# A gated scan and two MLPs on one core: the order of the SBUF tiles, and with it the offset at which each one begins

## The chip, the cores and the metric

The kernel runs on one core of a Trainium2 chip. The metric is the time of one execution on the device in microseconds (us), the median of repeated runs. SBUF, the memory that the engines read from and write to, has 128 partitions; a tile has the same address in each of them, and an address here is a number of bytes from the beginning of a partition.

## The reference

`x` and `f_logit` are `[2, 6080, 256]`; taken as rows there are 12160 tokens of 256 numbers. The weights are `[256, 2048]` and `[2048, 256]` for each of two MLPs, all in float32.

```python
def reference(x, f_logit, lower_bound, w_in1, w_out1, w_in2, w_out2):
    f = lower_bound + (1 - lower_bound) * sigmoid(f_logit)
    for t in range(S):                       # a scan along the 6080 tokens
        h = f[:, t] * h + (1 - f[:, t]) * x[:, t]
        y[:, t] = h
    x = y.reshape(12160, 256)
    x = square(relu(x @ w_in1)) @ w_out1     # first MLP
    return elu(x @ w_in2) @ w_out2           # second MLP
```

## The kernel before

**Precision.** Each float32 operand of a product is split into a high part and a low part, and a product is made of three matmuls: high weights with high data, high weights with low data, low weights with high data. Each of these is one load of 128x128 weights (the stationary operand, a run of 128 float32, 512 bytes, in each partition) and one matmul that streams 512 columns of data past them (the moving operand, 2048 bytes in each partition; 384 or 448 columns at some places near the beginning). The program has 8688 such pairs.

**Units and runs.** The tokens are cut into units, the first two smaller than the rest, which have 1024 tokens in two halves of 512. A run is one MLP on one unit; the first MLP of a unit goes two units ahead of the second. A run has eight slots, one for each eighth of the hidden dimension. From the third unit on, a slot has seven products for two halves of tokens and two halves of the hidden slice, with sums and differences of data and weights in place of the eighth product:

- `add_first`: three products, 9 matmuls, with weights from a tile `ws` and data from a tile `xa`;
- `add_later`: four products, 12 matmuls, with weights from `ws` and data from a tile `xb`;
- `add_out`, twice: 12 matmuls each (line 855), with weights from `wo0` or `wo1` (the output weights of the two MLPs, which stay in SBUF from the beginning) and data from a tile `g`.

The matmuls of `add_first` and `add_later` have one line in the profile, 633. The first two units of the first MLP are "plain": four products of 3 matmuls each for a half, with weights that lie alternately in a `ws` tile and in an `s` tile (`plain_weights`, line 321).

**Other engines.** Between the matmuls, ScalarE (ACT) and VectorE (DVE) copy products out of PSUM, add them, apply the activation and split the result into the parts in `g` (lines 652 to 678, 756 to 807). DVE also does the scan (line 602) and what leads to it (lines 575 to 589). The weights are split once, in the first quarter of a millisecond, and are kept in DRAM (`wd`); `ws` is reloaded from there for each slot (line 472). All DMAs but the very first go through the queue of SyncE.

**Order.** The class `Order` is a planner: it simulates the steps with fixed costs and writes them out, engine by engine. It knows nothing of addresses.

**Addresses.** Pools get their space in the order in which they are opened (lines 178 to 194), from low addresses to high. At the bottom lie 1024 bytes of scratch and four constants, a 32-byte place for each, up to byte 1152. Then come the two buffers of `ws` (7168 bytes each), then the pool `const` with five small tiles (`lb`, `ga`, `gb`, `carry`, `warm`, one 32-byte place each) and with `wo0` and `wo1` (32768 bytes each), then all the others. The sizes of all large tiles are multiples of 512 bytes. So all of them behind the small ones have the same remainder when their address is divided by 512, and so have all the slices of weights and of data that matmuls read, since these begin at multiples of 512 bytes in their tiles.

Of the kernel before, what the change touches and what calls it, by code (L numbers as in the profile page):

```python
# [7 lines left out]
F32 = mybir.dt.float32  # L8
F32R = mybir.dt.float32r
# [6 lines left out]
P = 128  # L16
HN = 512
CN = 256
SIZES = ((512, 384), (512, 512))
LEAD = 2  # L20
BEHIND = 2
AGE = 8.0
ROW = 1 / 2240
# [3 lines left out]
BUFS = {  # L27
# [3 lines left out]
}  # L31
# [119 lines left out]
def kernel(  # L151
# [12 lines left out]
    B, S, D = x.shape  # L164
# [3 lines left out]
    KF = DFF // P  # L168
# [6 lines left out]
    PLAIN = len(SIZES)  # L175
    starts = [sum(map(sum, units[:u])) for u in range(NU)]

    pools = {"ws": ctx.enter_context(tc.tile_pool(name="ws_pool", bufs=BUFS["ws"]))}
    const = ctx.enter_context(tc.tile_pool(name="const", bufs=1))
    lb = const.tile([P, KD], F32, name="lb")  # L180
    ga = const.tile([P, KD], F32, name="ga")
    gb = const.tile([P, KD], F32, name="gb")
    carry = const.tile([P, KD], F32, name="carry")
    warm = const.tile([P, 1], F32, name="warm")
    wo = [const.tile([P, KF, 2, D], F32R, name=f"wo{m}") for m in range(2)]
    pools |= {
        tag: ctx.enter_context(tc.tile_pool(name=f"{tag}_pool", bufs=n))
        for tag, n in BUFS.items()
# [27 lines left out]
    def slots_of(m, u):  # L216

        if not plain(m, u):
            return [(m, u, None, g) for g in range(KG)]
        a, b = ([(m, u, h, g) for g in range(KG)] for h in range(2))  # L220
        got = a[:LEAD]
        for i in range(LEAD, KG + LEAD):
            got += a[i : i + 1] + b[i - LEAD : i - LEAD + 1]
        return got

    runs = [(0, u) for u in range(BEHIND)]
    for u in range(BEHIND, NU):
        runs += [(1, u - BEHIND), (0, u)]
    runs += [(1, u) for u in range(NU - BEHIND, NU)]
    slots = [s for r in runs for s in slots_of(*r)]  # L230
# [25 lines left out]
    for s in slots:  # L256
        m, u, h, g = s
# [702 lines left out]
    for kind, s in pe_order:  # L960
# [3 lines left out]
        m, u, h, g = s  # L964
        if kind != "later" and s == first_of[m, u]:
            if m == 0:
                keys = {}
                before = slots_of(0, u - 1)
                for hh in range(2):
                    due = in_due[(m, u, hh, 0) if plain(m, u) else s]  # L970
                    for q in range(2):
                        k = before[SCANS[2 * hh + q] * len(before) // KG] if u >= BEHIND else None
                        keys[hh, q] = add_scan(n_scan, u, hh, q, due - 6.0 + 2.0 * (q - 1), n_first[k] if k else None)
# [43 lines left out]
```

## Time and profile before

| | us |
|---|---|
| median of 3 runs | 2049.47 (2049.08 to 2049.62) |
| profiled execution, its own time | 2049.94 |
| its span, first to last instruction | 2048.2 |
| TensorE (PE) busy | 1995.6 |
| weight loads (PEld) busy | 1633.5 |
| VectorE (DVE) busy | 1676.1 |
| ScalarE (ACT) busy | 1638.2 |

The busy time of PE is the time in which at least one matmul is under way; consecutive matmuls overlap, so it doesn't say how fast they follow one another. That is read from a timeline: from the start of a block of matmuls to the start of the next block, divided by the number of matmuls in it. In the timeline used below, the second column of a row (the block's length) runs to the end of its last matmul and overlaps with the next block; the first column is the one to subtract.

### The profile page before, as it was taken

How to read it: one execution, taken by the hardware profiler on the slowest of the kernel's cores; microseconds unless marked ns; L12 is line 12 of the kernel's file. 1: busy time of each engine (PE TensorE's matmuls, PEld its weight loads, DVE VectorE, ACT ScalarE, POOL GpSimd, SP SyncE). 2: the span in 40 equal slices, each digit the busy share in tenths (PEclk: the TensorE clock that was granted, in tenths of full speed). 3: DMA queues.
4: the chain of work that ended last, by engine and by line, in shares of the span. 5: the costliest groups of instructions: out<-in, count | busy, mean ns of one | idle time of the engine just before them, and what ended most of it. 6: DMA issues, size and time to landing. Idle time of an engine off the chain costs nothing.

```text
span 2048.2 us, 24509 instructions
## 1 busy us (share of the span) xinstructions
PE 1995.6 (97%) x8688; PEld 1633.5 (80%) x8688; DVE 1676.1 (82%) x2285; ACT 1638.2 (80%) x2170; POOL 0.2 (0%) x4
## 2 busy tenths in 40 slices
PE   5999969999999999999999999999999999999998
PEld 4887958888888888888888888888888888888886
DVE  6878997788889779879878888977987987857886
ACT  6988967887888788888788788878888878878885
POOL 0000000000000000000000000000000000000000
PEclk9999989999999999999999999999999999999999
DMA  7877744324324334333432432433433333233231
GB/s 191 240 245 241 230 129 128 131 91 142 125 94 137 99 132 131 111 131 114 128 131 90 143 125 93 137 99 131 132 110 132 114 108 131 91 111 118 94 105 54
DMA packets 235138, 267.30 MB, mean 131 GB/s; under 512 B 160008, under 2 KB 160776, under 8 KB 235016
## 3 DMA queue, kind: packets, MB, share of 16 engines
q1 hardware_dynamic: 234432, 265.21, 41.3%
q8 instruction: 68, 1.11, 0.2%
q10 hardware_dynamic: 584, 0.53, 0.1%
q14 instruction: 54, 0.44, 0.1%
HBM read 221.91 MB, written 43.78 MB: 130 GB/s over the span
## 4 chain that ended last, share of the span: by engine, by line
PE 90%; DVE 4%; ACT 2%; DMA 2%; issue 1%; SPq 1%; DVEq 0%; ACTq 0%
PE a L855 47%; PE c L633 43%; DVE g L678 1%; DMA a<-rd 1%; DMA fs<-in_f_logit_dram 1%; ACT g L673 1%; SPq L566 0%; ACT r L658 0%; ACT a L369 0%; DMA st<-in_moe_w_in_dram 0%; ACT r L725 0%; DVE a L375 0%; DVE a L378 0%; DVE F L602 0%; DVE a L339 0%
## 5 line engine op out<-in xcount | busy, mean ns | idle before, releaser
L855 PE MATMUL a<-g,wo 128*128 128x512 f32 (+1 forms) x4608 | 1107.1, 389 | 0.9 <-DVE g L678 0.9
L855 PEld LDWEIGHTS a<-g,wo 128*128 128x128 f32 x4608 | 865.2, 188 | 184.5 <-DVE g L678 1.3
L678 DVE TENSOR_TENSOR g<-r,g 128x1024 fp32r<-128x1024 f32 (+2 forms) x384 | 463.2, 1206 | 169.4 <-ACT g L673 168.4
L633 PE MATMUL c<-xb,ws 128*128 128x512 f32 (+2 forms) x2208 | 540.4, 393 | 0.0
L673 ACT ACTIVATE g<-r 128x1024 fp32r<-128x1024 f32 (+2 forms) x384 | 403.4, 1050 | 134.7 <-PE a L855 121.8
L633 PEld LDWEIGHTS c<-xb,ws 128*128 128x128 f32 x2208 | 414.7, 188 | 94.2
L633 PE MATMUL c<-xa,ws 128*128 128x512 f32 (+1 forms) x1680 | 427.6, 398 | 44.2 <-ACT xa L482 35.7
L633 PEld LDWEIGHTS c<-xa,ws 128*128 128x128 f32 x1680 | 318.1, 190 | 122.1 <-ACT xa L482 36.1
L756 ACT ACTIVATE s<-c 128x512 f32<-128x512 f32 (+1 forms) x528 | 307.3, 588 | 7.3 <-PE c L633 7.3
L668 DVE SCALAR_TENSOR_TENSOR r<-e,r 128x1024 f32<-128x1024 f32 (+1 forms) x192 | 232.1, 1209 | 34.3 <-ACT e L665 34.3
L662 ACT ACTIVATE e<-r 128x1024 f32<-128x1024 f32 (+1 forms) x192 | 201.5, 1049 | 39.8 <-DVE r L800 37.0
L658 ACT ACTIVATE r<-r 128x1024 f32<-128x1024 f32 x192 | 201.7, 1051 | 2.3
L665 ACT ACTIVATE e<-e 128x1024 f32<-128x1024 f32 (+1 forms) x192 | 201.4, 1049 | 1.5
L796 ACT ACTIVATE r<-c 128x512 f32<-128x512 f32 (+1 forms) x176 | 104.0, 591 | 106.1 <-PE c L633 106.0
L760 DVE TENSOR_TENSOR s<-s 128x512 f32<-128x512 f32 (+1 forms) x176 | 119.9, 681 | 74.2 <-ACT s L756 74.0
L793 DVE TENSOR_TENSOR s<-c,s 128x512 f32<-128x512 f32 (+1 forms) x176 | 120.6, 685 | 39.9 <-PE c L633 38.9
L804 DVE TENSOR_TENSOR r<-c,s 128x512 f32<-128x512 f32 (+1 forms) x176 | 119.5, 679 | 4.4
L800 DVE TENSOR_TENSOR r<-c,s 128x512 f32<-128x512 f32 (+1 forms) x176 | 119.8, 680 | 2.2
L807 DVE TENSOR_TENSOR r<-s 128x512 f32<-128x512 f32 (+1 forms) x176 | 119.1, 677 | 0.0
L652 ACT ACTIVATE r<-r 128x1024 f32<-128x1024 f32 x80 | 84.4, 1055 | 3.5 <-DVE r L807 3.5
L655 ACT ACTIVATE r<-r 128x512 f32<-128x512 f32 x80 | 50.4, 630 | 30.7 <-DVE r L800 30.7
L602 DVE TENSOR_TENSOR_SCAN F<-fT,carry,xT 128x256 f32<-128x256 f32 (+2 forms) x94 | 65.3, 723 | 1.2
(47 smaller groups left out, 759.0 us busy)
## 6 DMA issues: line engine op xcount, KB each, us to landing
ws<-wd SPq DMA_DIRECT2D x176, 896.0 KB, 4.9
fs<-in_f_logit_dram SPq DMA_DIRECT2D x184, 64.0 KB, 2.4
xs<-in_x_dram SPq DMA_DIRECT2D x184, 64.0 KB, 2.5
xd<-o SPq DMA_DIRECT2D x46, 256.0 KB, 4.3
F<-xd SPq DMA_DIRECT2D x22, 512.0 KB, 5.0
out_dram<-o SPq DMA_DIRECT2D x88, 128.0 KB, 2.8
st<-in_moe_w_out_dram SPq DMA_DIRECT2D x16, 512.0 KB, 5.5
wd<-wp SPq DMA_DIRECT2D x24, 256.0 KB, 3.6
```

Of the source, the lines that this page charges most:

```text
L633: nc.tensor.matmul(out, lhsT=ws[:, p, w], rhs=xs[:, r, v], start=start and q == 0, stop=stop and q == 2, skip_group_check=check,)
L658: nc.scalar.activation(r_t[0], r_t[0], AF.Square)
L662: nc.scalar.activation(t["e"], r_t[0], AF.Relu, scale=-1.0)
L665: nc.scalar.activation(t["e"], t["e"], AF.Exp, scale=-1.0)
L668: nc.vector.scalar_tensor_tensor(r_t[0], t["e"], 1.0, r_t[0], op0=ALU.subtract, op1=ALU.max)
L673: nc.scalar.activation(g_t[s, which][:, 0], r_t[0], AF.Copy)
L678: nc.vector.tensor_tensor(g_t[s, which][:, 1], r_t[0], g_t[s, which][:, 0].bitcast(F32), op=ALU.subtract)
L756: nc.scalar.activation(t["s"][:, c - 1], t[c], AF.Copy)
L760: nc.vector.tensor_tensor(t["s"][:, 1], t["s"][:, 1], t["s"][:, 2], op=ALU.add)
L793: nc.vector.tensor_tensor(t["s"][:, 0], t[0], t["s"][:, 0], op=ALU.add)
L800: nc.vector.tensor_tensor(odd[0][:, 1], t[2], t["s"][:, 0], op=ALU.add)
L855: nc.tensor.matmul(a, lhsT=y, rhs=v, start=begin and jj == 0 and p == 0, stop=end and jj == len(mine) - 1 and p == 2, skip_group_check=True,)
```

## The change

The order in which the pools are opened is changed, and a tile of 56 float32 (224 bytes) that nobody uses is added behind the small constants. `wo0` and `wo1` get a pool of their own.

```diff
+GAP = 56
...
-    pools = {"ws": ctx.enter_context(tc.tile_pool(name="ws_pool", bufs=BUFS["ws"]))}
     const = ctx.enter_context(tc.tile_pool(name="const", bufs=1))
     lb = const.tile([P, KD], F32, name="lb")
     ga = const.tile([P, KD], F32, name="ga")
     gb = const.tile([P, KD], F32, name="gb")
     carry = const.tile([P, KD], F32, name="carry")
     warm = const.tile([P, 1], F32, name="warm")
-    wo = [const.tile([P, KF, 2, D], F32R, name=f"wo{m}") for m in range(2)]
+    const.tile([P, GAP], F32, name="gap")
+    pools = {"ws": ctx.enter_context(tc.tile_pool(name="ws_pool", bufs=BUFS["ws"]))}
+    outer = ctx.enter_context(tc.tile_pool(name="outer", bufs=1))
+    wo = [outer.tile([P, KF, 2, D], F32R, name=f"wo{m}") for m in range(2)]
```

The addresses in the two built programs, with the remainder by 512 in brackets:

| tile | before | after |
|---|---|---|
| small tiles | 15488 to 15616 | 1152 to 1280 |
| `ws`, two buffers | 1152 (128), 8320 (128) | 1536 (0), 8704 (0) |
| `wo0`, `wo1` | 15648 (288), 48416 (288) | 15872 (0), 48640 (0) |
| `xa`, `xb` (data of line 633) | 113952 (288), 126240 (288) | 114176 (0), 126464 (0) |
| `g`, two buffers (data of line 855) | 167200 (288), 175392 (288) | 167424 (0), 175616 (0) |
| `s`, two buffers | 183584 (288), 189728 (288) | 183808 (0), 189952 (0) |
| all other large tiles | (288) | (0) |

Apart from addresses the two programs are the same: the same instructions stand in the same order on every engine and every queue.

## Rows read from the trace of the kernel before

**Rows 1.** The page: busy time by engine; granted clock; the chain's shares by engine.
```profile
PE 1995.6 (97%) x8688; PEld 1633.5 (80%) x8688; DVE 1676.1 (82%) x2285; ACT 1638.2 (80%) x2170; POOL 0.2 (0%) x4
...
PEclk9999989999999999999999999999999999999999
...
PE 90%; DVE 4%; ACT 2%; DMA 2%; issue 1%; SPq 1%; DVEq 0%; ACTq 0%
```

**Rows 2.** Busy time by stretch: length, engines, then clock, DMA share, GB/s.
```profile
core 0: us, PE busy (x) PEld busy (x) DVE busy (x) ACT busy (x) POOL busy (x), PEclk, DMA share, GB/s
...
37.50:262.00 224.50, 221.54 (x1045) 192.90 (x1044) 189.58 (x319) 197.13 (x311) 0.00 (x0) 1.00 0.77 233
262.00:287.00 25.00, 8.02 (x21) 5.79 (x21) 24.88 (x44) 12.71 (x18) 0.00 (x0) 0.59 0.40 102
287.00:2033.50 1746.50, 1746.50 (x7565) 1420.65 (x7564) 1429.15 (x1866) 1408.23 (x1811) 0.00 (x0) 1.00 0.37 117
```

**Rows 3.** Waits from 287 to 2028: us in total, times, longest.
```profile
ACT g L673 <- PE a L855: 117.8, 185, 2.2
ACT r L796 <- PE c L633: 105.5, 123, 1.1
...
ACT fs L570 <- DMA fs<-in_f_logit_dram: 2.0, 4, 0.6
```

**Rows 4.** Timeline of PE, one slot from 1003.80: start, length, what.
```profile
1003.80 2.97 PE L633 MATMUL c<-xb,ws 128*128 128x512 f32 x12
1006.61 2.90 PE L855 MATMUL a<-g,wo 128*128 128x512 f32 x12
1009.34 2.26 PE L633 MATMUL c<-xa,ws 128*128 128x512 f32 x9
1011.44 2.92 PE L855 MATMUL a<-g,wo 128*128 128x512 f32 x12
1014.20 2.97 PE L633 MATMUL c<-xb,ws 128*128 128x512 f32 x12
```

**Rows 5.** The same view in the plain units, from 75 to 107.
```profile
75.37 2.25 PE L633 MATMUL c<-xb,ws 128*128 128x384 f32 x12
77.46 2.26 PE L855 MATMUL a<-g,wo 128*128 128x384 f32 x12
...
85.04 2.27 PE L633 MATMUL c<-xb,s 128*128 128x384 f32 x12
87.15 2.24 PE L855 MATMUL a<-g,wo 128*128 128x384 f32 x12
...
98.26 2.97 PE L633 MATMUL c<-xa,ws 128*128 128x512 f32 x12
101.07 2.89 PE L855 MATMUL a<-g,wo 128*128 128x512 f32 x12
103.80 2.88 PE L633 MATMUL c<-xa,s 128*128 128x512 f32 x12
106.52 2.27 PE L855 MATMUL a<-g,wo 128*128 128x384 f32 x12
```

**Rows 6.** Weight loads grouped by shape: busy us, mean ns of one; idle before.
```profile
L855 PEld LDWEIGHTS a<-g,wo 128*128 128x128 f32 x4608 | 865.2, 188 | 184.5 <-DVE g L678 1.3
...
L633 PEld LDWEIGHTS c<-xb,ws 128*128 128x128 f32 x2208 | 414.7, 188 | 94.2
```

**Rows 7.** The longest wait of PE between 225 and 290.
```profile
PE c L633 <- ACT xa L482: 15.1, 1, 15.1
```

**Rows 8.** Busy time by stretch, columns as above: the length of one run.
```profile
784.00:867.00 83.00, 83.00 (x360) 67.48 (x360) 72.80 (x107) 66.24 (x88) 0.00 (x0) 1.00 0.44 127
```

**Rows 9.** DMA issues of plain weights into the two tiles: count, KB, us to landing.
```profile
ws<-wd SPq DMA_DIRECT2D x4, 512.0 KB, 5.1
s<-wd SPq DMA_DIRECT2D x4, 512.0 KB, 4.9
```

## The prediction

> **What bounds the kernel now.** I read the page first. TensorE is busy for 97% of the span and makes 90% of the chain that ended last, at the full granted clock nearly throughout [rows 1]. So the second question is where it is not the bound, and the table by stretches answers it [rows 2]. [...] From 262.00 to 287.00 PE works for 8.02 us of 25.00 and DVE for 24.88 [rows 2], and PE stands still for 15.1 us in one wait for data in `xa` [rows 7]: there the work of DVE and the transfers ahead of it set the time.
>
> So a change of this kernel that touches no instruction can do something worth measuring in one way only: the matmuls of the long stretch follow one another faster or slower. The third view is therefore the timeline of PE, and from it the distance from start to start. In one slot [rows 4], 12 matmuls with weights from `ws` take 1006.61 - 1003.80 = 2.81 us, the next 12 with weights from `wo` 2.73, then 9 with `ws` 2.10, then 12 with `wo` 2.76. The slot has 45 matmuls and takes 10.40 us. Per matmul that is 234, 228, 233 and 230 ns. [...]
>
> **What the rows say of addresses.** The decisive comparison is in the plain units [rows 5], where the same data tile `xa` meets weights in two tiles. 12 matmuls of 512 columns with weights in `ws` take 101.07 - 98.26 = 2.81 us; 12 with weights in `s` take 106.52 - 103.80 = 2.72. Instruction, number of columns, data and clock are the same. What differs is where the weights lie: `ws` at remainder 128 by 512, `s` at 288, which is also the remainder of `xa`. The `wo` blocks, whose weights lie at 288 like their data in `g`, are near 2.72 as well (2.73 between 101.07 and 103.80). So in every block of 512 columns that I compare, weights and data with equal remainders give about 227 ns a matmul, unequal ones about 234. The weight load itself is not longer: 188 ns on average from `wo` and 188 from `ws` [rows 6]. It is the matmul beside which the load for the next one runs that takes longer. That looks like two streams out of the same memory, whose steps meet or miss one another by the difference of their addresses.
>
> Two details fit that reading. A `wo` block that follows a `ws` block starts slow: 2.76 against 2.73 in the two halves of the same slot [rows 4], as if the two streams needed a few matmuls to fall back into step. And at 384 columns the difference is gone: 2.09 us for `ws` (77.46 - 75.37), 2.11 for `s` (87.15 - 85.04) [rows 5]. A matmul of another length meets the load at other moments. So this is no fixed fee for reading the tile `ws`.
>
> **The change, part by part.** It removes and adds no instruction, and moves none on any queue; the unused tile costs 224 bytes per partition. Three things can come of the new addresses.
>
> *Weights in `ws`.* Their difference from the data goes from -160 to 0, the same as `wo` and `g` have had. I take the pace of the `s` block, 2.72 us for 12, since `s` is filled by the same kind of transfer and meets the same data. For the slot of rows 4: the `ws` block of 12 gives 2.81 - 2.72 = 0.09 us, that of 9 gives 2.10 - 9/12 x 2.72 = 0.06. The two `wo` blocks no longer follow blocks that are out of step and give 0.01 and 0.04. Sum: 0.20 of 10.40 us, so a slot of 10.20.
>
> *How often.* The stretch of 1746.50 us holds 1746.50 / 10.40 = 168 slots. 168 x 0.20 = 33.6 us.
>
> *Absolute addresses.* All tiles go from 288 (or 128) to 0. No row shows weights and data that both lie at 0. The nearest rows are those with both at 288. If only the difference counts, nothing more comes of it. [...]
>
> *Before 287 us.* The matmuls there become faster too, but PE is not what the end waits for: it stands for 15.1 us at one place [rows 7], and a faster PE only stands longer. I book 0. The upper bound is 1045 matmuls of the stretch 37.50 to 262.00 [rows 2] at (2.81 - 2.72) / 12 us, 7.8 us, if all of it counted. The transfers land at new addresses too; 512 KB into `ws` at 128 took 5.1 us and into `s` at 288 took 4.9 [rows 9], so an offset is worth 0.2 us of a transfer at most, and 0 on average. I book 0, with a few us of a chain of DMAs on either side in the range. DVE and ACT read and write the same number of elements; I book 0 for them.
>
> *What is late next.* PE gets 1.9% faster, and the planner reckoned with 512/2240 = 0.2286 us for a matmul, so PE will go slightly ahead of the plan where it was slightly behind. A run of 83.00 us has 72.80 us of DVE work and 66.24 of ACT work [rows 8]; after the change it has 83.00 x 10.20/10.40 = 81.4 us for them. DVE is then at 89%. ACT's waits for PE (117.8 and 105.5 us [rows 3]) are the cover, about 1.3 us in a slot of 10.4, and the 0.20 us come out of that. So most of the gain should stay.
>
> The profiled execution took 2049.94 us, its span 2048.2. 2049.94 - 33.6 = 2016.3; the median stands 0.47 below that execution, so 2015.9, rounded to 2016.
>
> **The rivals.** *No change (2049.5).* The pace could be a property of the tile and not of its remainder: `ws` is the lowest tile in memory, and its layout differs (seven weights in a row instead of four). Against it: `ws` is not slower at 384 columns. [...] Chance 0.08.
>
> *Slower (2071).* What counts could be the weights' own address and not the difference: a load from a multiple of 64 bytes (`ws` at 128) would collide, one from 288, which lies 32 bytes off such a multiple, would not. Then the change puts every weights tile where only `ws` was. The place is `wo` in the long stretch: its two blocks in a slot go from 2.73 and 2.76 to 2.81, 0.08 + 0.05 = 0.13 us, in 168 slots 21.8 us, so 2049.5 + 21.8 = 2071. It decides if the blocks of line 855 come out at 2.81. Against it: at 384 columns, weights from `ws` at 128 are as fast as any. Chance 0.06.
>
> *Half of it (about 2033).* The streams fall into step, but DVE, at 89% of a run, or a chain from a product to `g`, is late in some slots and PE waits. If half is lost: 2049.5 - 16.8 = 2032.7. For it: some waits of DVE and ACT on each other in the long stretch are already of the order of 1 us. Against it: PE never waits there now. Chance 0.09.
>
> *More (under 2006).* [...] Chance 0.03.
>
> **How the numbers follow.** The forecast, 2016, with its own spread of 2006 to 2026 (7.8 us more from the beginning and a little from transfers on one side; on the other up to 10 us of the 33.6 lost to blocks that still start out of step or to short new waits), has 0.74. The rest: half 0.09, no change 0.08, slower 0.06, more 0.03. For 8 in 10 I need the forecast's own range and two thirds of the half case: 2006 to 2034. About 0.2%, 4 us, is what a measurement of this kernel can tell from no change. Faster by more: 0.74 + 0.09 + 0.03 = 0.86; within: 0.08; slower: 0.06.
>
> **What the profile after should show.** In the long stretch, blocks of 12 matmuls of 512 columns at 2.72 us from start to start whatever the weights tile, 9 in 2.04, and a slot of 10.20. PE is still busy all the time between some 287 and 2000 us. The stall before 287 us stays about as long, and weight loads stay at 188 ns. The step on addresses is wrong if `ws` blocks stay at 2.81 with `wo` blocks unchanged (no change) or if `wo` blocks rise to 2.81 (slower). The step on the cover is wrong if blocks are at 2.72 but PE waits for ACT or DVE appear behind 287 us.

## The result and the profile after

The changed kernel takes 2016.66 us, median of 4 runs (2015.62 to 2018.06), against 2049.55 (2049.08 to 2051.31) for the kernel before, run beside it: 32.9 us less, a ratio of 0.9838 with a 95% interval of 0.9821 to 0.9855. The forecast was 2016, with 2006 to 2034. A second pairing, in five rounds, gave 2016.90 and 2049.08, a ratio of 0.9844 (0.9831 to 0.9858).

The page after, in the part that answers to [rows 1]: busy time by engine. The line numbers are three higher now (636 was 633, 858 was 855).

```profile
PE 1964.0 (97%) x8688; PEld 1630.8 (81%) x8688; DVE 1674.3 (83%) x2285; ACT 1638.0 (81%) x2170; POOL 0.2 (0%) x4
```

Only PE has lost busy time to speak of, 31.6 us; DVE and ACT work as long as they did, to within 2 us. PE is still the bound in the long stretch, as in [rows 2]; here its row in the table by stretches of the kernel after (length, busy time of PE, PEld, DVE, ACT, POOL, then the granted clock).

```profile
287.00:2000.00 1713.00, 1713.00 (x7552) 1416.22 (x7551) 1426.21 (x1865) 1405.84 (x1809) 0.00 (x0) 1.00 0.37 119
```

What has changed is the pace. The timeline of PE after, one slot as in [rows 4] (start, length, what; it is the starts that are subtracted):

```profile
999.84 2.88 PE L636 MATMUL c<-xb,ws 128*128 128x512 f32 x12
1002.56 2.88 PE L858 MATMUL a<-g,wo 128*128 128x512 f32 x12
1005.28 2.20 PE L636 MATMUL c<-xa,ws 128*128 128x512 f32 x9
1007.32 2.88 PE L858 MATMUL a<-g,wo 128*128 128x512 f32 x12
1010.04 2.88 PE L636 MATMUL c<-xb,ws 128*128 128x512 f32 x12
```

2.72, 2.72, 2.04 and 2.72 us, a slot of 10.20: every block of this slot has the pace of the `s` block of [rows 5], 226.7 ns a matmul. The weight loads have not become shorter (grouped by shape, as in [rows 6]: count, busy us, mean ns):

```profile
L858 PEld LDWEIGHTS a<-g,wo 128*128 128x128 f32 x4608 | 864.8, 188 | 173.8 <-DVE g L681 1.3 <-issue 0.2
```

The stall before the long stretch is as long as it was in [rows 7] (waits from 225 to 290):

```profile
PE c L636 <- ACT xa L485: 15.1, 1, 15.1
```

The waits of the long stretch (287 to 2000; us in total, times, longest), as in [rows 3]: the cover (ACT's waits for PE) has shrunk, and there is a new row in which the weight load waits.

```profile
ACT g L676 <- PE a L858: 88.8, 152, 1.2
...
PEld c L636 <- DVE r L807: 3.6, 10, 0.4
```

PE has no wait of its own in this view, but the ten waits of the load reach the matmuls behind it. The timeline of PE at one of them shows a block of 9 with `ws` that takes 2.25 us in place of 2.04; its slot, from 601.35 to 611.78, is 10.43 long:

```profile
606.79 2.41 PE L636 MATMUL c<-xa,ws 128*128 128x512 f32 x9
609.04 2.90 PE L858 MATMUL a<-g,wo 128*128 128x512 f32 x12
```

Of 166 slots between the first and the last `xb` block of the stretch, 153 take 10.20 us after the change and ten take 10.43.

### The profile page after: what moved, and what is told of

It reads as the page before. It is cut to its first block, busy times and chain, and to the rows that moved or that the text cites. A ratio compares the mean times of both kernels' runs of the same rounds, so it can differ in the third digit from the quotient of the medians.

```text
span 2014.8 us, 24509 instructions
## 1 busy us (share of the span) xinstructions
PE 1964.0 (97%) x8688; PEld 1630.8 (81%) x8688; DVE 1674.3 (83%) x2285; ACT 1638.0 (81%) x2170; POOL 0.2 (0%) x4
## 4 chain that ended last, share of the span: by engine, by line
PE 88%; DVE 4%; ACT 3%; DMA 2%; issue 1%; SPq 1%; ACTq 0%; DVEq 0%
PE a L858 47%; PE c L636 41%; DVE g L681 1%; DMA a<-rd 1%; DMA fs<-in_f_logit_dram 1%; ACT g L676 1%; ACT r L728 1%; ACT r L661 1%; SPq L569 0%; ACT a L372 0%; DVE a L378 0%; ACT st L375 0%; DVE a L381 0%; DMA st<-in_moe_w_in_dram 0%; DVE F L605 0%
## 5 line engine op out<-in xcount | busy, mean ns | idle before, releaser
L636 PE MATMUL c<-xb,ws 128*128 128x512 f32 (+2 forms) x2208 | 525.7, 387 | 0.0
L636 PE MATMUL c<-xa,ws 128*128 128x512 f32 (+1 forms) x1680 | 419.3, 393 | 43.0 <-ACT xa L485 35.0
```

What stands on the lines that cost most here:

```text
L636: nc.tensor.matmul(out, lhsT=ws[:, p, w], rhs=xs[:, r, v], start=start and q == 0, stop=stop and q == 2, skip_group_check=check,)
```

## The experiments

### Is it the difference of the addresses, or the addresses themselves?

The theory of the prediction: what counts is the difference between the address of the weights and that of the data. Rivals: each tile has to lie at a multiple of 512; or weights at a multiple of 64 are slow; or `ws` as such is slow. Three kernels were made for this.

**Only `ws` moved.** The pools in the new order but without the gap. `ws` comes to remainder 288, and all other large tiles stay at exactly the addresses of the kernel before.

```diff
-GAP = 56
...
-    const.tile([P, GAP], F32, name="gap")
```

> The small constants first, as in the change, but without the gap: ws comes to remainder 288, and every other large tile stays at exactly the address it has in the kernel before (288). Theory (the difference decides): the whole gain, 2016 to 2017 us, with blocks of 12 at 2.72 us. Rival (multiples of 512 as such): no gain, 2049.5, as no large tile lies at such a multiple. Rival (weights at a multiple of 64 are slow): 2016 as well, since nothing is at one now.

Measured: 2017.76 us, median of 4, ratio 0.9851 (0.9834 to 0.9867), 0.8 above the range expected. Within the intervals the whole gain is there though no large tile lies at a multiple of 512. A slot in its timeline of PE is 10.20 long:

```profile
1008.27 2.88 PE L634 MATMUL c<-xb,ws 128*128 128x512 f32 x12
...
1018.47 2.88 PE L634 MATMUL c<-xb,ws 128*128 128x512 f32 x12
```

So it isn't the multiple of 512. Of the change's three steps (constants first, the gap, a pool for `wo`) the first is enough for the pace.

**`ws` back at its old difference, all others at 0.** Two pads on the changed kernel, one below `ws` and one behind it.

```diff
-GAP = 56
+GAP = 56 + 88
...
+    outer.tile([P, 40], F32, name="back")
```

> All large tiles at multiples of 512 as in the change, except ws, which lies at remainder 352: the difference to its data is the -160 that it had in the kernel before. Theory (the difference decides): all of the gain is gone, 2049 to 2050 us, ws blocks of 12 at 2.81 us. Rival (weights at a multiple of 64 are slow): ws is off such a multiple and fast, wo is at one and slow, some 2038 us (wo blocks 2.81, ws blocks 2.72). Rival (only alignment to 512 counts, for each tile by itself): wo blocks keep 2.72 and ws blocks are slow, 2049 us too, so this run tells the theory apart from the second only.

Measured: 2047.35 us, median of 10, beside 2048.69 for the kernel before, ratio 0.9994 (0.9985 to 1.0003). That is 1.7 below the range expected and 1.3 below the kernel before; the interval has no difference in it too, and the shorter end that came with `o` at 0 (below, 1.1 us) is of this size. The gain of the long stretch is gone, and the slot has its old pattern:

```profile
1011.87 2.97 PE L637 MATMUL c<-xb,ws 128*128 128x512 f32 x12
1014.68 2.89 PE L859 MATMUL a<-g,wo 128*128 128x512 f32 x12
1017.41 2.26 PE L637 MATMUL c<-xa,ws 128*128 128x512 f32 x9
...
1022.27 2.97 PE L637 MATMUL c<-xb,ws 128*128 128x512 f32 x12
```

2.81 us for the `ws` block, 2.73 for the `wo` block behind it and 10.40 for the slot: [rows 4] again, to the last digit, with every absolute address of a large tile another. `wo` lies at a multiple of 64 here and is not slow, so that rival falls too.

**A curve of offsets.** A kernel that has nothing but matmuls, so that each case stands alone: blocks of 96 pairs, weights tiles at remainders 0 to 480, the data at 0 (`xzero`), then at 288 (`xoff`).

```python
...
for xt in (xz, xo):
    for r in range(0, 512, 32):
        block(w[r], 0, xt, 512)        # 32 groups of three matmuls, as in the kernel
for n in (448, 384):
    for r in range(0, 512, 32):
        block(w[r], 0, xz, n)
...
```

> Only matmuls, and none of the reference's work: 96 pairs of weight load and matmul in a row for each of 16 weights tiles, whose remainder by 512 goes from 0 to 480 in steps of 32, first against a data tile at remainder 0 (512 columns), then against one at 288 (512 columns), then at 0 with 448 and with 384 columns; at the end weights that begin 0, 4, 8, 16 and 32 bytes behind a multiple of 512. Theory (the difference of the two addresses by 512 decides): a block of 96 takes 96 x 0.2267 = 21.76 us where the difference is 0 and 96 x 0.2341 = 22.47 us where it is 352 (-160), and the row of times against data at 288 is the row against data at 0, moved by 288: fast for weights at 288, slow for 128. Rival (a multiple of 512 as such is good): against data at 288 no block is as fast as 21.76. Rival (weights at a multiple of 64 are slow): 0, 64, 128 ... slow and 32, 96 ... fast against both. Rival (the tile ws itself): all blocks equal. At 384 columns the theory has little or no difference between remainders 0 and 352 (16.7 us each).

Its timeline of PE, data at 0 first, then at 288; the name `w128x` says that the weights have remainder 128:

```profile
98.80 22.64 PE L35 MATMUL c<-xzero,w96x 128*128 128x512 f32 x96
121.28 22.47 PE L35 MATMUL c<-xzero,w128x 128*128 128x512 f32 x96
...
165.99 22.15 PE L35 MATMUL c<-xzero,w192x 128*128 128x512 f32 x96
187.97 22.56 PE L35 MATMUL c<-xzero,w224x 128*128 128x512 f32 x96
210.37 21.93 PE L35 MATMUL c<-xzero,w256x 128*128 128x512 f32 x96
232.13 22.55 PE L35 MATMUL c<-xzero,w288x 128*128 128x512 f32 x96
...
477.49 22.64 PE L35 MATMUL c<-xoff,w128x 128*128 128x512 f32 x96
499.96 22.47 PE L35 MATMUL c<-xoff,w160x 128*128 128x512 f32 x96
...
589.05 21.93 PE L35 MATMUL c<-xoff,w288x 128*128 128x512 f32 x96
610.82 22.55 PE L35 MATMUL c<-xoff,w320x 128*128 128x512 f32 x96
...
1057.24 16.80 PE L35 MATMUL c<-xzero,w0x 128*128 128x384 f32 x96
1073.88 16.81 PE L35 MATMUL c<-xzero,w32x 128*128 128x384 f32 x96
...
1241.77 17.12 PE L35 MATMUL c<-xzero,w352x 128*128 128x384 f32 x96
1258.73 17.06 PE L35 MATMUL c<-xzero,w384x 128*128 128x384 f32 x96
```

From start to start: 22.48 us for weights at 96, 21.98 at 192 and 21.76 at 256; of the others 128 takes 22.30, and 32, 64, 160 and 224 take 22.4. Against data at 288, weights at 288 take 21.77, and weights at 128 (the case of the kernel before) 22.47, which is 234.1 ns a matmul. The row goes with the difference. A difference of 256 is as good as 0, which was not foreseen: for 512 columns the row repeats after 256 bytes, not 512 (22.48 us at 96 and 22.47 at 352, 21.98 at 192 and 21.99 at 448). One part of the expectation failed: at 384 columns the remainders 0 and 352 take 16.64 and 16.96 us, 3.3 ns a matmul apart, not the same. And at 448 columns 0 isn't the best: in the same timeline weights at 96 take 822.49 - 803.27 = 19.22 us, at 0 19.46 and at 256 19.83.

### Does the curve carry over to the kernel?

Two more places for `ws`, all other tiles at 0, made with pads as above (`GAP = 56 + 64` and `56 + 48`).

> All large tiles at multiples of 512 as in the change, but ws at remainder 256. Theory (only the difference by 256 counts, as the curve of offsets has 21.76 at 256 as at 0): the whole gain, 2016 to 2018 us. Rival (the difference by 512 counts in the kernel): 2049.

> All large tiles at multiples of 512, but ws at remainder 192, where the curve of offsets has 21.98 to 22.00 us for 96 matmuls, some 2.3 ns a matmul above the floor. Theory (the curve carries over to the kernel): 21 ws matmuls in a slot at 2.3 ns and up to 0.05 us for wo blocks that fall back into step, times 168 slots: 8 to 17 us above the change, 2025 to 2034 us. Rival (any difference but 0 by 256 costs the whole): 2049.

Measured: 2015.84 us at 256 (ratio 0.9837, 0.9821 to 0.9854), and 2025.71 at 192 (ratio 0.9884, 0.9870 to 0.9899). At 256 it is the whole gain (0.2 below the range expected), at 192 it lies in the range. At 192 a `ws` block of 12 takes 2.75 us (timeline of PE):

```profile
1004.91 2.91 PE L637 MATMUL c<-xb,ws 128*128 128x512 f32 x12
1007.66 2.88 PE L859 MATMUL a<-g,wo 128*128 128x512 f32 x12
...
1015.16 2.91 PE L637 MATMUL c<-xb,ws 128*128 128x512 f32 x12
```

The slot is 10.25 long; 0.05 us in 168 slots are 8.4 us, and the run is 9.0 us above the changed kernel, 9.9 above the one with `ws` at 256, which ran beside it.

### Is there a better difference than 0, and what meets what?

**Steps of 4 bytes.** The same kind of kernel, one block of 96 for each difference from 0 to 252.

> Only matmuls, none of the reference's work: 96 pairs of weight load and matmul (512 columns) for each difference between weights and data from 0 to 252 bytes in steps of 4. Theory (the difference by 256 sets where the load's and the data's addresses meet in time): 21.76 to 21.80 us at 0 and 16, about 22.4 at 32, 64, 160 and 224, 22.47 at 96, 22.3 at 128 and 22.0 at 192, as the steps of 32 gave, with smooth or repeating values between. [...] Rival: some difference that no pool can give by chance lies under 21.76 and would be a better choice than 0.

No block of its 64 is under 21.76 us (the smallest difference of starts), so for loads of 128 columns and 512 columns of data nothing quicker was found in steps of 4 bytes. But the smooth or repeating curve is not there. Differences of 100 and 228 are as quick as 0 here, and the slowest block is the one at 164, with 979.29 - 956.50 = 22.79 us, 237 ns a matmul. A difference of 16 bytes takes 154.54 - 132.14 = 22.40 us here:

```profile
132.14 22.56 PE L33 MATMUL c<-xzero,w16x 128*128 128x512 f32 x96
154.54 22.56 PE L33 MATMUL c<-xzero,w20x 128*128 128x512 f32 x96
```

In the curve of offsets the same 16 bytes, as a slice 4 elements into `w0x`, came behind another block and took 1453.39 - 1431.62 = 21.77:

```profile
1431.62 21.93 PE L35 MATMUL c<-xzero,w0x 128*128 128x512 f32 x96
1453.39 5.76 PE L35 MATMUL c<-xzero,w480x 128*128 128x512 f32 x24
```

So at some differences there are two paces that hold for a whole block. What picks one is not shown: the block before it is another in the two runs, and so is the distance of the two tiles, with the same remainders. At differences of 0 and 256 every block of 96 with loads of 128 columns and 512 columns of data, but for the one that opens the curve of offsets, took 21.76 to 21.80 us, whatever its neighbour.

**Shorter loads, and bfloat16.** Weights of 64 and 32 columns instead of 128 with the same 512 columns of data; then 128 columns with everything in bfloat16.

> Only matmuls, none of the reference's work: 96 pairs for each of eight differences (0 to 224 in steps of 32), first with float32 weights of 128 columns as before, then of 64 and of 32 columns (a shorter load, 256 and 128 bytes), the data always 512 columns; then all in bfloat16. Theory (the load of the next weights meets the data stream while it runs): the shorter load meets it less; at difference 96, where 128 columns give 7.4 ns a matmul above the floor of 226.7, 64 columns give some 4 and 32 columns 2 or less. Rival (the excess belongs to the hand-over from one matmul to the next and not to the load's run): 7 ns at any length. In bfloat16 load and data are half as many bytes; the theory says that a difference should still show if the two run at comparable paces, and none if the load is over quickly; its size is open.

```profile
211.04 22.25 PE L36 MATMUL c<-xzero,w0x 128*64 128x512 f32 x96
233.12 22.40 PE L36 MATMUL c<-xzero,w32x 128*64 128x512 f32 x96
...
277.69 21.95 PE L36 MATMUL c<-xzero,w96x 128*64 128x512 f32 x96
299.48 22.18 PE L36 MATMUL c<-xzero,w128x 128*64 128x512 f32 x96
...
410.03 23.15 PE L36 MATMUL c<-xzero,w32x 128*32 128x512 f32 x96
433.02 22.40 PE L36 MATMUL c<-xzero,w64x 128*32 128x512 f32 x96
...
566.51 20.89 PE L36 MATMUL c<-xhalf,h0x 128*128 128x512 bf16 x96
587.24 20.88 PE L36 MATMUL c<-xhalf,h32x 128*128 128x512 bf16 x96
```

The expectation of an excess that shrinks with the load fell. At a difference of 96 itself it is 0.3 ns a matmul with 64 columns and 3.9 with 32 (477.39 - 455.26 = 22.13 us), where some 4 and 2 or less were expected. With 64 columns a difference of 0 takes 22.08 us and 96 takes 21.79: good and bad have changed places. With 32 columns the worst block of all appears, 22.99 us (239.5 ns) at 32. So the excess does not shrink with the length of the load, and "the load's run meets the data" is too simple; nor is it a fixed 7 ns, as the rival had it. In bfloat16 the eight differences are alike, 20.72 or 20.73 us from start to start, 215.8 ns a matmul: no dependence on the difference in these steps of 32, and 11 ns less than the best of float32.

### What else changed, and a version that is faster still

**The kernel before, once more,** for the profile's own spread.

> The kernel before, unchanged, for a second profile. In the changed kernel the last long stretch of PE begins some 1.5 us earlier than before and the piece behind the last matmul is 1.1 us shorter; the pace of matmuls explains neither. Theory (these are differences from run to run in transfers): the second profile of the same kernel moves the same two places by 1 us or more. Rival (the new addresses quicken the transfers): both places stay within 0.3 us of the first profile.

Its span is 2046.5 us, 1.7 below the first profile of the same kernel. The rows that bound its long stretch and its end, against the same places after (timeline of PE: a block at full clock, and the last block that waits; then the last issues of SyncE's queue). First the kernel before, second profile:

```profile
288.26 2.59 PE L855 MATMUL a<-g,wo 128*128 128x448 f32 x12
2033.48 5.51 PE L855 MATMUL a<-g,wo 128*128 128x512 f32 x23 [0.86 <-DVE g L678]
2038.41 5.16 SPq L901 DMA_DIRECT2D out_dram<-o  x8
```

Then the kernel after:

```profile
288.46 2.59 PE L858 MATMUL a<-g,wo 128*128 128x448 f32 x12
2002.91 5.51 PE L858 MATMUL a<-g,wo 128*128 128x512 f32 x23 [0.86 <-DVE g L681]
2007.84 4.37 SPq L904 DMA_DIRECT2D out_dram<-o  x8
```

The stretch was 1745.22 us and is 1714.45, 30.8 less. The beginning differs by 0.2; between the two profiles of before it differs by 1.8 (290.04 and 288.26), so the theory of chance holds there. At the end it does not: from the last wait to the end of the span it was 2046.5 - 2033.48 = 13.0 us and is 2014.8 - 2002.91 = 11.9, and the issue of the last eight stores took 5.16 and takes 4.37. The first profile of before has 13.1 and 5.18. In the kernel in which only `ws` moved, whose `o` stays at 288, the issue takes 5.14:

```profile
2006.08 5.14 SPq L902 DMA_DIRECT2D out_dram<-o  x8
```

With `o` at 0 and `ws` at 256 (`ws_256_rest_0`) it takes 4.38. From the start of this issue to the end of the span it is 8.1 us in both profiles of before and 2014.3 - 2006.08 = 8.2 us with only `ws` moved, at the new pace; it is 2014.8 - 2007.84 = 6.96 after and 2014.7 - 2007.65 = 7.05 with `ws` at 256. So this gain goes with the place of `o` and not with the pace.

The DMA issues by kind (count, KB, us to landing) show where that comes from: those in pieces of 256 bytes (64 numbers of one token; lines 564 to 566 and 899 to 901 of the kernel before). Only `ws` moved:

```profile
out_dram<-o SPq DMA_DIRECT2D x88, 128.0 KB, 2.8
```

After:

```profile
out_dram<-o SPq DMA_DIRECT2D x88, 128.0 KB, 2.3
```

2.8 to 2.3 us for a store and, in the same views, 2.4 to 2.1 for a load into `fs`, and this time the absolute address counts: `fs` and `o` go from 288 to 0 by the gap alone. Why pieces at 288 land later is not shown.

**The planner's rate.** The plan still holds PE to 228.6 ns a matmul.

```diff
-ROW = 1 / 2240
+ROW = 1 / 2259
```

> The changed kernel with one number of the planner changed: the rate at which it lets PE work, 1/2259 us per column (226.7 ns for 512) in place of 1/2240 (228.6), so that its plan has the pace that the blocks now have. Theory (the short waits of PE on DVE and ACT that came with the change, some 2 us in the long stretch, stem from a plan that is late by 2 ns a matmul): 1 to 2 us less, 2014 to 2016. Rival (the order in which DVE and ACT work is what it is, and a new order can as well be worse): no difference or some us more.

> The changed kernel as it is, as the partner of the next run on the same chip: 2016 to 2017 us.

> The changed kernel with the planner's rate of 1/2259 us per column once more, in more rounds. Its first run was 2013.7 us, though the long stretch of PE had the same length and the same short waits as with 1/2240. Theory (another order before 287 us and at the end makes it shorter there): 2 to 4 us under its partner again. Rival (chance between calls): no difference beyond 1 us.

Measured: 2013.69 us (2012.59 to 2014.18), ratio 0.9824 (0.9808 to 0.9841); and, once more, beside its partner 2014.01 (2011.89 to 2014.15) against 2016.90 (2015.02 to 2019.22), ratios to before 0.9827 (0.9813 to 0.9840) and 0.9844 (0.9831 to 0.9858). The runs of the two kernels don't overlap, the intervals of the ratios do; some 3 us less is likely, and it is the quickest version here. But not for the reason given. The new wait of the load in the long stretch has stayed, ten times and 3.5 us. Most of what it gained lies ahead of that stretch: the first matmul behind the stall starts at 275.25 us in its timeline of PE, where the changed kernel has 278.23. In the profiles of the second pair it is 274.44 and 277.12, so some 2.7 to 3.0 us both times, while two profiles of one kernel differ by about 1 us there. Which of the moved steps does that was not tried.

```profile
275.25 0.80 PE L636 MATMUL c<-xa,ws 128*128 128x512 f32 x1 [15.54 <-ACT xa L485]
```

## Why the prediction was right, point by point

- **The bound.** Right. PE has no slack from 287 us on, and a quicker PE made the whole stretch shorter, by 30.8 us. One reading was incomplete: the longest row of the waits before, DVE waiting 157.1 us for ACT, is not in [rows 3]. DVE isn't the bound, so nothing hangs on it.
- **The difference, not the address.** Right, and shown from both sides: equal remainders off the multiple of 512 give the gain (`only_ws_moved`), all tiles but one at multiples of 512 don't (`ws_352_rest_0`). The choice of 2.72 us, a pace measured with equal remainders at 288, for a case that no row showed was the step that could have failed.
- **The comparison it was read from.** It held less than the prediction read in it. The `ws` block at 98.26 in [rows 5] stands behind a block of 384 columns (at 96.18, in the same view) and the `s` block at 103.80 behind one of 512, so the place of the weights was not all that differed. After the change the block in the place of that at 98.26 takes 2.76 us with all differences at 0, and the `s` block that follows takes 2.72 (104.41 - 101.69); another `s` block there, behind 384 columns, takes 2.77 (80.28 - 77.51).

```profile
96.21 2.92 PE L636 MATMUL c<-xa,ws 128*128 128x512 f32 x12
98.97 2.88 PE L858 MATMUL a<-g,wo 128*128 128x512 f32 x12
```

So 0.05 of the 0.09 us went with the address there, and 0.04 with the block ahead. The sum isn't touched: it goes by blocks that stand behind 512 columns [rows 4], and these went from 2.81 to 2.72. The detail of a `wo` block that starts slow behind `ws` was misread as well, since both `wo` blocks of a slot, 2.73 and 2.76, stand behind `ws`; both came down to 2.72, as booked.

- **The size.** The slot became 10.20 us, as summed. 168 x 0.20 = 33.6 us was the term for the stretch; it measured 30.8. Most of the 2.8 us that are missing are the ten slots of 10.43, 10 x 0.23 = 2.3 us. The rest is open.
- **The cover.** Right in the main: ACT's waits for PE for its `g` buffers fell from 117.8 to 88.8 us, as a smaller cover should. But the sign that the prediction named for a wrong cover did show in ten slots: there the weight load waits for DVE, 3.6 us in total, and 2.3 of them reach PE. These were booked at nothing in the forecast itself and stood in its spread, as short new waits.
- **Transfers.** Booked at 0, measured at 1.1 us at the end. The step that failed is the row taken for it: [rows 9] shows 512 KB transfers in pieces of 2048 bytes (line 469 of the kernel before), and what went with the address were those in pieces of 256 bytes, 2.8 us for a store of 128 KB from 288 and 2.3 from 0.
- **The nearness.** That the median came within 0.7 us of the forecast is in part luck: 2.8 us less in the stretch and 1.1 us more at the end partly cancel, and 30.8 + 1.1 = 31.9 leaves 1 us of the 32.9 to the beginning, where two profiles of one kernel differ by more than that.
- **The detail at 384 columns.** The conclusion that `ws` is no slow tile was right. The reading behind it was wrong in part: in blocks of 96 matmuls 384 columns do differ, 16.64 against 16.96 us, which is 2.08 and 2.12 for 12. The blocks of 12 in [rows 5], 2.11 for `s` and 2.09 for `ws`, are neither of them at their own pace. For `s` the block of 512 columns ahead is a likely reason, as with the 2.76 above; for `ws` it is open.
- **The rivals.** No change fell by the curve: 21.76 to 22.48 us with nothing but addresses changed. Slower fell with `wo` at 0 and 2.72 us. Half had its mechanism, but for 2.3 us and not for 16.8. More (under 2006, chance 0.03) fell with the pace, which stayed at 226.7 ns; no run shows a block of float32 matmuls of 512 columns with a lower one.

What stays open is the mechanism inside the chip. That the difference decides for loads of 128 float32 columns is shown in steps of 32 bytes (a block of 96 takes 21.76 us at a difference of 256, 22.48 at 96), and for 512 columns of data that 256 is as good as 0; why it does, and why with loads of 64 columns 96 (21.79 us) is better than 0 (22.08), is not.

## What to carry to other kernels

Where TensorE is the bound with float32 operands, read the distance from start to start of blocks that differ in one tile only; here some 4 ns a matmul were worth 30.8 us, in a stretch in which PE waited for nothing. Compare blocks that stand behind the same kind of block. For loads of 128 columns and 512 columns of data put weights and data at the same remainder by 256 bytes (226.7 ns a matmul here, 229.0 to 234.2 at the other steps of 32), which costs only the order of the pools, and look at the timeline, since with another length of load or of data another difference was better (96 against 0: 21.79 and 22.08 us with loads of 64 columns, 19.22 and 19.46 with 448 columns of data). Tiles that DMAs fill or empty in pieces of 256 bytes were better off at remainder 0 than at 288, the only two that were tried (2.1 against 2.4 us for `fs`, 2.3 against 2.8 for `o`).

## What the runs showed of the hardware that was not expected

- The pace of float32 pairs goes with the difference of weights and data addresses: 226.7 ns at 0 and 256, 229 at 192, 234.2 at 96, and 237 at 164 in the run with steps of 4 bytes (128 load columns, 512 data columns).
- At a difference of 16 bytes two paces hold, 226.8 ns in one run and 233.3 in another.
- At equal remainders 12 matmuls of 512 columns take 2.76 us behind a block of 384 columns and 2.72 behind one of 512.
- In bfloat16 it is 215.8 ns at all eight differences tried.
- A store of 128 KB in pieces of 256 bytes lands in 2.3 us from tiles at a multiple of 512, in 2.8 from remainder 288.
